# Spread maxima by one product with the unit matrix, and the PSUM places divided anew at tile 32: an attention and MLP kernel on one core

## The chip, the core and the metric

The kernel runs on one core of a Trainium2 chip. A core has TensorE (PE in the rows; PEld is its weight load), VectorE (DVE), ScalarE (ACT), GpSimd (POOL) and SyncE (SP, which here only starts transfers), each with a queue of its own in fixed order, an on-chip memory of 128 partitions, and PSUM, 8 banks of 128 x 512 fp32 values into which TensorE writes. The metric is the time of one execution on the device in microseconds (us), lower is better; the time given is the median of several executions.

## The reference, cut to what matters

```python
def _attn_ref(q, k, v, w1, b1, w2):        # q, k, v: 4 x 8 x 576 x 64
    scores = scale * np.matmul(q, k.transpose(0, 1, 3, 2))
    rel = pos[:, None] - pos[None, :]
    x = (np.log1p(abs(rel)) / np.log1p(np.maximum(pos[:, None], 1.0)))[..., None]
    bias = np.maximum(x @ w1 + b1, 0.0) @ w2          # one table for all 4 batches
    scores = scores + bias.transpose(2, 0, 1)[None, :, :, :]
    attn = softmax(scores)
    return np.matmul(attn, v)

def _moe_ref(x, w_in, w_out):               # x: 2304 x 512, w_in: 512 x 2048
    h = x @ w_in
    g = h * np.clip(h + 3.0, 0.0, 6.0) / 6.0
    return g @ w_out
```

`reference` runs the attention, lays its heads side by side and runs the MLP. The weights `w_in` and `w_out` come as 64-bit floats.

## The kernel before

**Pieces of work.** The four batches and the eight heads (four pairs) are cut into units: `(b, p, 0)` for rows 0 to 255 and `(b, p, 1)` for rows 256 to 575; a unit has four or five tiles of 128 rows by 576 columns. The main loop counts tiles with `n`, 144 in all. A tile is a product of q and k into PSUM (`qk_step`, L518 on, tile name s_ps), a VectorE pass that adds the bias and finds the row minimum (`soft_max`, L564), a ScalarE exponential (L575), and a transposition of the result. For the first 32 tiles (batches 0 and 1, rows 0 to 255, called direct) all of this is fp32 and TensorE transposes (t_ps, L623, copied out at L626). From tile 32 on the result is split into two fp16 halves (`soft_norm`, `soft_low`, hl) and a DMA transposes. At the end of a unit comes the product with v (pv_ps, L665 direct with its row sums at L676, else L711) and the copy into `x`.

**The MLP.** For each batch and row half, `ffn` (from L741) makes 16 hidden blocks (h_ps, L786, 12 products each) with ScalarE (t, L776), VectorE (t, L769), ScalarE and GpSimd (g, L763 and L765) behind them, and then 4 output blocks (o_ps, L809, 48 products each, copied out at L819). Both weight matrices are first turned from 64-bit floats into two fp16 halves by VectorE, ScalarE and GpSimd: `w_in_prep` in the first 90 us, `w_out_prep` from about 99 us. `w_out_prep` has eight chunks, and on each VectorE makes three passes over 128 x 1024 values (L265, L268, L271) and for most chunks a fourth (L141). Some chunks are staged in `z_e`, which the bias table's work also uses: a group of 16 rows of the bias table is made by `z_group` (L851 on VectorE, L855 on ScalarE), `bias_mm` (b_ps, L868) and `bias_out` (L884).

**The maxima.** Six scales are powers of two from a maximum over all 128 partitions: four for v (one per batch), one for `w_in` and one for `w_out`. `spread_max` (L145 on) finds them: a maximum per partition (m, L147, for v also masked at L150), a TensorE transposition of that column into one row (m_ps, L153), a VectorE maximum over the row (g, L155), a TensorE product of a row of ones with that one value, which gives it to all partitions (L157), and a VectorE copy (p, L160). Between these steps stand three `yield`s, so that other work is issued between. The one of `w_out` is issued at once (`drain` in `pack`). Its result gives `r_w2c` (L221), by which all 16 blocks of the first batch half's `g` are multiplied (L122 and L124) before the first output block.

**PSUM.** Two pools: places "s" of two banks each (`s_bank`, for s_ps and t_ps, and b_ps at first) and places "w" of one bank (`w_bank`, for h_ps, o_ps, pv_ps, m_ps). At first there are three s and two w. `open_banks` (from L1126) closes them and opens two s and four w over the same banks; each new place waits for the old tiles that lay there. From then on b_ps takes two w places, and `w_bank` makes sure that an output block still open is finished before the fourth claim after it.

**The order of the work.** The program is written down in source order, tile by tile: `front(n)` issues the softmax, the weights' and the bias table's steps and the MLP's steps at rates given in `CFG`. The framework that builds the program then orders the instructions of each engine by its own model of when each can start, with the source order as priority, and puts in the waits. From tile 39 on (`SWITCH`; `open_steady`, L1132) TensorE keeps the source order itself; there the steps that are left of the first MLP half are issued at once, and `open_banks` is called, since `CFG['psw']` is 99. From tile 45 on SP keeps the source order too. Tile 21 (`START`) opens the first MLP half.

Of the kernel before, what the change touches and what calls it, by code (L numbers as in the profile page):

```python
# [10 lines left out]
F32 = mybir.dt.float32  # L11
# [4 lines left out]
ALU = mybir.AluOpType  # L16
AX = mybir.AxisListType
# [7 lines left out]
NG = S // 16  # L25
CQ = 2.0 ** -25
VC = 5 * 128
CFG = {'z0': 'AD', 'gz': 12, 'z1': 'AD', 'gz2': 16, 'zeng': 'DDA', 'sg': 'P', 'wm1': 'A', 'wm2': 'RRAAAAAA', 'hl': 'AP', 'gl': 'PP', 'vm': 'A', 'g0': 8, 'rwi': 2.0, 'rw0': 0.3, 'rw1': 0.7, 'ro': 0.85, 'rb': 1.7, 'rf0': 1.3, 'rf': 2.0, 'rf1': 1.55, 'la': 6, 'gq': 2, 'gap': 0.0, 'wu': 8, 'act': 'o', 'g1': 2, 'w64': 5, 'rfo': 2.3, 'tv': 'A', 'pw': 0, 'po': 0, 'gr': 'AD', 'wb': 3, 'fb': 2, 'spn': 45, 'sw': 39, 'ws': 2, 'kn': 10, 'kw': 1, 'os': 11, 'ro2': 2.0, 'bo': 12, 'rb0': 1.5, 'psw': 99, 'xp': 0, 'mw': 2, 'he': 0}
F64_BIAS = 2.0 ** -112
F64_MAX = float(np.uint32(0x0FEFFFFF).view(np.float32))  # L30

# [2 lines left out]
def attention_moe_kernel(  # L34
# [16 lines left out]
    nc = tc.nc  # L51
    cfg = CFG
    tc.cur_priority = 10000
# [5 lines left out]
    const = ctx.enter_context(tc.tile_pool(name="const", bufs=1))  # L59
# [30 lines left out]
    def w_bank(name):  # L90

        if name == "o_ps":
            out_open[:] = [True, 0]
        elif out_open[0] and four[0]:
            while out_open[0] and out_open[1] == 3:
                next(queue[0])
            out_open[1] += 1
        return pools["ps_w"].tile([128, 512], F32, tag="w", name=name)

    open_psum(stack_p, 3, 2)  # L100
    eye_sb = const.tile([128, 128], F32, name="eye_sb")
# [2 lines left out]
    wo = big.tile([128, 2, KF, DM], F16, name="wo")  # L104
    bias_d = [dr_p.tile([H, min(128, S - i), S], F32, name=f"bias{i}") for i in range(0, S, 128)]

    ones_sb = const.tile([1, 128], F32, name="ones_sb")
    b1_sb = const.tile([128, 1], F32, name="b1_sb")
    w2_sb = const.tile([128, 32], F32, name="w2_sb")
    tq = [const.tile([128, 2, 128], F32R, name=f"tq{r}") for r in range(2)]  # L110
# [34 lines left out]
    def spread_max(parts, name, mask=False):  # L145
        m = const.tile([128, 1], F32, tag="m", bufs=2, name=f"m_{name}")
        nc.vector.tensor_reduce(out=m, in_=parts, op=ALU.max, axis=AX.X)  # L147
        if mask:
            mb = m.bitcast(U32)
            nc.vector.tensor_single_scalar(out=mb, in_=mb, scalar=0x7F800000, op=ALU.bitwise_and)  # L150
        yield
        ps = w_bank("m_ps")
        nc.tensor.transpose(ps[0:1, 0:128], m, eye_sb)  # L153
        g = const.tile([1, 1], F32, tag="gm", bufs=2, name=f"g_{name}")
        nc.vector.tensor_reduce(out=g, in_=ps[0:1, 0:128], op=ALU.max, axis=AX.X)  # L155
        yield
        nc.tensor.matmul(out=ps[:, 128:129], lhsT=ones_sb, rhs=g)  # L157
        yield
        p = const.tile([128, 1], F32, name=f"p_{name}")
        nc.vector.tensor_copy(out=p, in_=ps[:, 128:129])  # L160
        return p

    def to_pow2(p):
# [4 lines left out]
    def v_scale(b):  # L168
        parts = const.tile([128, PAIRS], F32, tag="vparts", name="vparts")
        for p in range(PAIRS):  # L170
            if b:
                t = st_p.tile([128, VC], F32, tag="vs", bufs=2, name="va")
            elif p < 2:
                t = v_t[0, p, 0] = v_p.tile([128, VC], F32, tag="vh", name="vf")
            else:
                t = v_t[0, p, 0] = st_p.tile([128, 1024], F32, tag="st", name="vf")[:, 0:VC]
            with behind():
                dq("v").dma_start(out=t, in_=vp[b, p])
            yield
            nc.vector.tensor_reduce(  # L180
                out=parts[:, p:p + 1], in_=t, op=ALU.max, axis=AX.X, apply_absolute_value=True
            )
        p = yield from spread_max(parts, f"v{b}", mask=True)
        to_pow2(p)
        s = const.tile([128, 1], F32, name=f"s_v{b}")
        nc.vector.reciprocal(out=s, in_=p)
        pscale[f"v{b}"] = (p, s)
# [28 lines left out]
    def row_ratio(p, name):  # L216
        pm = yield from spread_max(p, name)
        rm = const.tile([128, 1], F32, name=f"rm_{name}")
        nc.vector.reciprocal(out=rm, in_=pm)
        r = const.tile([128, p.shape[1]], F32, name=f"r_{name}c")  # L220
        nc.vector.tensor_scalar(out=r, in0=p, scalar1=rm, scalar2=None, op0=ALU.mult)  # L221
        pscale[name] = pm
        pscale["r" + name[1]] = r
# [807 lines left out]
    nc.sync.dma_start(out=eye_sb, in_=eye)  # L1031
    nc.sync.dma_start(out=T[:, 0:512], in_=ltab[:, 0:512])
    nc.vector.memset(cv_sb, 0.0)
    nc.vector.memset(ones_sb, 1.0)
    nc.vector.memset(c36[:, 0:1], 3.0 * CQ)
    nc.vector.memset(c36[:, 1:2], 6.0 * CQ)
    for r in range(2):
# [1 line left out]
    for cs in (slice(512, LT), slice(0, 512)):  # L1039
        nc.vector.tensor_scalar(  # L1040
            out=T[:, cs], in0=T[:, cs], scalar1=w1_sb, scalar2=None, op0=ALU.mult
# [164 lines left out]
def _layout(q, k, v, w1, b1, w2, moe_w_in, moe_w_out):  # L1206
# [7 lines left out]
    qkd = _np.concatenate([kd, qd], axis=5).reshape(Bn, PAIRS, 2, 128, HALF + 256)  # L1214
    qkd = qkd.transpose(0, 1, 3, 2, 4).reshape(Bn, PAIRS, 128, 512 + S)[:CFG["fb"]]
    rows = _np.arange(128)[:, None] + 128 * _np.arange(5)[None, :]
# [44 lines left out]
```

## Time and profile before

| | us |
|---|---|
| median of 3 executions | 697.87 (696.44 to 702.76) |
| the profiled execution | 696.51 |
| its span, first to last instruction | 694.5 |
| busy in the span: PE, PEld | 638.2, 453.0 |
| busy in the span: DVE, ACT, POOL | 485.6, 487.7, 261.7 |

Busy time of TensorE is the sum of the time in which a product runs; the granted clock (PEclk) is the share of full speed that TensorE had in a stretch, 1.00 being 2.4 GHz and 0.50 being 1.2 GHz. "Idle before" is time in which an engine did nothing ahead of an instruction, and the arrow names what ended it.

### The profile page before, as it was taken

Reading aid. Unit: us, or ns where it says so; the run is one execution under the profiler, and the core shown is the slowest. Engines: PE = TensorE matmul, PEld = TensorE weight load, DVE = VectorE, ACT = ScalarE, POOL = GpSimd, SP = SyncE. Lnnn points to the kernel's source line nnn. Section 1 sums busy time; section 2 is a strip of 40 time slices with the busy share of each in tenths; the row PEclk is TensorE's granted clock in tenths of the full one; section 3 lists DMA queues with packets and bytes.
Section 4 is the critical chain, followed back from the end, with each engine's and each line's share of the span. In section 5 each row is a group of like instructions: output and inputs, shape, how many; then the busy total and the mean of one; then the engine's idle time right before and its main releaser. Section 6 shows DMA issues by size and latency. Waiting matters only on the chain. (4 is left out here: it accounts for less than half of the span.)

```text
span 694.5 us, 15117 instructions
## 1 busy us (share of the span) xinstructions
PE 638.2 (92%) x5558; PEld 453.0 (65%) x5558; DVE 485.6 (70%) x1157; ACT 487.7 (70%) x968; POOL 261.7 (38%) x322
## 2 busy tenths in 40 slices
PE   7677899875999989999899999999999999999998
PEld 2223456653687667677788778767776777777775
DVE  7889868899846977667868887777587757710310
ACT  7987778976747987688668867886588757721620
POOL 1112125765413442246335623563365424410420
PEclk9999999998899999999999999999999999999999
DMA  8898779742893989999999899869787895400000
GB/s 294 297 329 325 268 268 337 263 130 77 230 245 93 215 229 210 236 211 206 225 258 266 167 216 191 192 142 210 169 195 136 191 177 122 91 15 29 1 10 28
DMA packets 175737, 130.13 MB, mean 187 GB/s; under 512 B 137520, under 2 KB 144944, under 8 KB 174640
## 3 DMA queue, kind: packets, MB, share of 16 engines
q1 hardware_dynamic: 165872, 113.84, 65.4%
q10 hardware_dynamic: 9792, 15.34, 7.4%
q8 instruction: 43, 0.70, 0.4%
q14 instruction: 30, 0.25, 0.1%
HBM read 77.24 MB, written 15.34 MB: 133 GB/s over the span
## 5 line engine op out<-in xcount | busy, mean ns | idle before, releaser
L786 PE MATMUL h_ps<-x,wi 128*128 128x256 f16 (+1 forms) x1536 | 200.9, 288 | 7.6 <-DVE t L769 4.0
L809 PE MATMUL o_ps<-g,wo 128*128 128x256 f16 (+1 forms) x1536 | 195.7, 286 | 1.6 <-ACT g L763 1.0
L786 PEld LDWEIGHTS <-wi 128*128 128x128 f16 x1536 | 147.7, 98 | 58.1 <-issue 18.7
L809 PEld LDWEIGHTS <-wo 128*128 128x128 f16 x1536 | 147.2, 98 | 47.2 <-issue 10.0
L765 POOL TENSOR_TENSOR g<-t,g 128x256 f16<-128x256 f32 (+1 forms) x128 | 105.5, 834 | 153.8 <-ACT g L763 152.2
L575 ACT ACTIVATE bt<-bt,sm 128x576 f32<-128x576 f32 x144 | 110.4, 767 | 41.2 <-DVE sm L564 39.4
L141 DVE SCALAR_TENSOR_TENSOR hl<-bt,sm,hl 128x576 f16<-128x576 f32 x112 | 99.1, 896 | 20.8 <-POOL hl L118 12.8
L769 DVE SCALAR_TENSOR_TENSOR t<-t,t,h_ps 128x320 f32<-128x320 f32 (+1 forms) x112 | 55.8, 515 | 47.6 <-ACT t L776 46.4
L763 ACT ACTIVATE g<-t 128x256 f16<-128x256 f32 (+1 forms) x128 | 55.4, 439 | 36.3 <-DVE t L769 35.5
L564 DVE CUSTOM_DVE_ANT_0 bt<-s_ps,bt 128x576 f32<-128x576 f32 x88 | 64.5, 750 | 22.0 <-PE s_ps L552 14.7
L118 POOL TENSOR_SCALAR hl<-bt,sm 128x576 f16<-128x576 f32 x56 | 46.7, 835 | 80.1 <-ACT bt L575 18.7
L418 POOL TENSOR_TENSOR qkl<-st,qkh 128x576 fp32r<-128x576 f32 (+2 forms) x48 | 58.5, 1238 | 37.5 <-ACT qkh L411 30.3
L776 ACT ACTIVATE t<-h_ps,t,hr 128x320 f32<-128x320 f32 (+1 forms) x112 | 64.3, 586 | 7.2 <-PE h_ps L786 2.9
L819 ACT ACTIVATE ot<-o_ps,os 128x256 f32<-128x256 f32 (+1 forms) x32 | 15.9, 497 | 64.7 <-PE o_ps L809 57.5
L868 PE MATMUL b_ps<-z_e,w_sb 128*32 128x288 f32 x448 | 45.4, 430 | 15.3 <-POOL x L699 5.9
L583 DVE TENSOR_SCALAR sm<-sm 128x1 f32<-128x1 f32 x112 | 16.9, 151 | 46.5 <-ACT bt L575 46.2
L124 ACT ACTIVATE hl<-bt,sm 128x576 f16<-128x576 f32 x56 | 43.0, 769 | 7.4 <-DVE sm L587 4.5
L851 DVE TENSOR_SCALAR z_e<-T,nbp 128x576 f32<-128x576 f32 x69 | 40.9, 638 | 1.9 <-PE b_ps L868 1.7
L884 ACT ACTIVATE bo<-b_ps,cv_sb,isc 128x288 f32<-128x288 f32 (+1 forms) x52 | 35.0, 674 | 4.3 <-DMA bias<-bo 2.4
L868 PEld LDWEIGHTS b_ps<-z_e,w_sb 128*32 128x32 f32 x448 | 14.9, 111 | 34.2 <-ACT z_e L855 6.8
L258 POOL TENSOR_SCALAR w<-w 128x1024 f32<-128x1024 f32 x8 | 12.2, 1522 | 64.3 <-ACT wo L257 58.2
L855 ACT ACTIVATE z_e<-T,bp 128x576 f32<-128x576 f32 x43 | 32.4, 769 | 5.0 <-DVE bp L1043 2.8
(132 smaller groups left out, 895.9 us busy)
## 6 DMA issues: line engine op xcount, KB each, us to landing
bt<-bias SPq DMA_DIRECT2D x36, 576.0 KB, 5.5
bias<-bo ACTq DMA_DIRECT2D x36, 288.0 KB, 5.7
w<-in_w_in_dram SPq DMA_DIRECT2D x8, 1024.0 KB, 7.1
vs<-in_vp_dram SPq DMA_DIRECT2D x24, 320.0 KB, 5.2
st<-in_qk_dram SPq DMA_DIRECT2D x16, 448.0 KB, 4.0
wo<-in_w_out_dram SPq DMA_DIRECT2D x5, 1024.0 KB, 6.6
bt<-bias SPq DMA_DIRECT2D x16, 288.0 KB, 3.3
qk<-in_qkd_dram SPq DMA_DIRECT2D x8, 544.0 KB, 9.1
```

Of the source, the lines that this page charges most:

```text
L118: nc.gpsimd.tensor_scalar(out=out, in0=full, scalar1=scale, scalar2=1.0, op0=ALU.mult, op1=ALU.mult)
L141: nc.vector.scalar_tensor_tensor(out=out, in0=full, scalar=scale, in1=high, op0=ALU.mult, op1=ALU.subtract)
L418: nc.gpsimd.tensor_sub(out=lo[:, c:c + w], in0=t[:, c:c + w], in1=hi[:, c:c + w].bitcast(F32))
L564: nc.vector.tensor_tensor_reduce(out=halves(bt), in0=ps, in1=halves(src), op0=ALU.add, op1=ALU.min, scale=-0.125, scalar=3.0e38, accum_out ...
L575: nc.scalar.activation(out=bt, in_=bt, func=AF.Exp, scale=-1.0, bias=sm[:, 0:1], accum_out=total)
L763: nc.scalar.activation(out=g[:, 0], in_=uu, func=AF.Copy)
L765: e.tensor_sub(out=g[:, 1], in0=uu, in1=g[:, 0])
L769: nc.vector.scalar_tensor_tensor(out=t_t[f], in0=t_t[f], scalar=cols(f)[2], in1=h_t.pop(f)[:, 0:n], op0=ALU.min, op1=ALU.mult,)
L776: nc.scalar.activation(out=t_t[f], in_=h_t[f][:, 0:n], func=AF.Relu, scale=cols(f)[0], bias=cols(f)[1],)
L786: nc.tensor.matmul(out=h_t[f][:, 0:n], lhsT=wi[:, a, c, f * 128:(f + 1) * 128], rhs=x[:, e, c], start=(k == 0), stop=(k == 3 * KC - 1),)
L809: nc.tensor.matmul(out=ops[:, 0:n], lhsT=wo[:, a, f, e * 128:(e + 1) * 128], rhs=g_t[f][:, r], start=(f == 0 and a == 0 and r == 0), stop= ...
L868: nc.tensor.matmul(out=pss[a][32 * k:32 * k + 32, 0:HALF], lhsT=w2_sb, rhs=z[:, a * HALF:(a + 1) * HALF],)
```

## The change

`spread_max` is left with one TensorE step: the column of maxima, repeated over 128 columns as the weights, times the unit matrix, gives every partition the whole row, and VectorE takes its maximum straight into p. Transposition, the product with ones, the copy, the row of ones and two of the three `yield`s go. `psw` becomes 32, so that `open_banks` is called in `front(32)`, seven tiles ahead of `open_steady`; TensorE's source order still begins at tile 39.

```diff
-CFG = {..., 'rb0': 1.5, 'psw': 99, 'xp': 0, 'mw': 2, 'he': 0}
+CFG = {..., 'rb0': 1.5, 'psw': 32, 'xp': 0, 'mw': 2, 'he': 0}
...
-    ones_sb = const.tile([1, 128], F32, name="ones_sb")
...
         yield
+
         ps = w_bank("m_ps")
-        nc.tensor.transpose(ps[0:1, 0:128], m, eye_sb)
-        g = const.tile([1, 1], F32, tag="gm", bufs=2, name=f"g_{name}")
-        nc.vector.tensor_reduce(out=g, in_=ps[0:1, 0:128], op=ALU.max, axis=AX.X)
-        yield
-        nc.tensor.matmul(out=ps[:, 128:129], lhsT=ones_sb, rhs=g)
-        yield
+        nc.tensor.matmul(out=ps[:, 0:128], lhsT=m.to_broadcast([128, 128]), rhs=eye_sb)
         p = const.tile([128, 1], F32, name=f"p_{name}")
-        nc.vector.tensor_copy(out=p, in_=ps[:, 128:129])
+        nc.vector.tensor_reduce(out=p, in_=ps[:, 0:128], op=ALU.max, axis=AX.X)
         return p
...
-    nc.vector.memset(ones_sb, 1.0)
```

## Rows read from the trace of the kernel before

**Rows 1.** Busy time by stretch: busy us and instructions of each engine, clock, DMA
```profile
core 0: us, PE busy (x) PEld busy (x) DVE busy (x) ACT busy (x) POOL busy (x), PEclk, DMA share, GB/s
0.00:100.00 100.00, 77.08 (x572) 36.85 (x574) 82.42 (x192) 80.22 (x127) 15.06 (x18) 1.00 0.84 305
100.00:125.00 25.00, 23.97 (x184) 15.25 (x180) 22.54 (x52) 20.22 (x41) 14.45 (x13) 1.00 0.84 293
125.00:173.00 48.00, 32.97 (x255) 23.71 (x256) 44.66 (x102) 38.96 (x73) 30.11 (x26) 0.91 0.45 147
173.00:183.20 10.20, 10.20 (x59) 4.83 (x58) 9.00 (x28) 7.40 (x12) 4.86 (x3) 0.74 1.04 287
183.20:212.00 28.80, 28.80 (x282) 22.39 (x280) 14.96 (x32) 14.15 (x25) 5.19 (x6) 1.00 0.81 211
212.00:460.00 248.00, 235.31 (x2347) 183.86 (x2339) 192.17 (x465) 195.03 (x418) 111.36 (x150) 1.00 0.92 207
460.00:694.50 234.50, 229.91 (x1879) 166.08 (x1876) 119.83 (x292) 131.74 (x277) 80.66 (x109) 1.00 0.51 106
```

**Rows 2.** TensorE in order of time, 127 to 184: start, us, line, idle before
```profile
127.45 2.77 PE L786 MATMUL h_ps<-x,wi 128*128 128x256 f16 x12
...
153.49 0.54 PE L552 MATMUL s_ps<-qkh 64*128 64x288 f32 x4
...
160.85 4.16 PE L665 MATMUL pv_ps<-atf,vf 128*64 128x256 f32 x20 [2.20 <-DVE sm L583]
...
165.53 1.48 PE L786 MATMUL h_ps<-x,wi 128*128 128x256 f16 x12
172.87 1.18 PE L868 MATMUL b_ps<-z_e,w_sb 128*32 128x288 f32 x4 [5.86 <-POOL x L699]
173.98 0.37 PE L153 MATMUL m_ps<-eye_sb,m_w 128*1 128x128 f32 x1
...
176.35 2.38 PE L786 MATMUL h_ps<-x,wi 128*128 128x256 f16 x12
178.66 0.38 PE L157 MATMUL m_ps<-g_w,ones_sb 1*128 1x1 f32 x2
...
183.23 0.50 PE L809 MATMUL o_ps<-g,wo 128*128 128x256 f16 x3
```

**Rows 3.** VectorE in order of time, 131 to 212
```profile
131.08 0.76 DVE L564 CUSTOM_DVE_ANT_0 bt<-s_ps,bt 128x576 f32<-128x576 f32 x1 [2.85 <-PE s_ps L532]
...
136.65 0.74 DVE L564 CUSTOM_DVE_ANT_0 bt<-s_ps,bt 128x576 f32<-128x576 f32 x1
...
151.71 0.75 DVE L564 CUSTOM_DVE_ANT_0 bt<-s_ps,k 128x576 f32<-128x576 f32 x1
...
172.76 0.14 DVE L147 TENSOR_REDUCE m_w<-w2p 128x1 f32<-128x8 f32 x1
...
174.81 0.47 DVE L769 SCALAR_TENSOR_TENSOR t<-t,c,h_ps 128x256 f32<-128x256 f32 x1
175.20 0.27 DVE L155 TENSOR_REDUCE g_w<-m_ps 1x1 f32<-1x128 f32 x1
...
179.07 0.16 DVE L160 COPY p_w<-m_ps 128x1 f32<-128x1 f32 x1 [0.82 <-PE m_ps L157]
...
211.32 0.76 DVE L564 CUSTOM_DVE_ANT_0 bt<-s_ps,bt 128x576 f32<-128x576 f32 x1 [8.56 <-PE s_ps L552]
```

**Rows 4.** ScalarE in order of time, at the hidden block ahead of the last
```profile
168.52 0.55 ACT L776 ACTIVATE t<-h_ps,c,hs 128x256 f32<-128x256 f32 x1
```

**Rows 5.** The instructions on m_ps: ns min/median/max, first and last start, forms
```profile
L157 PE MATMUL m_ps<-g_v,ones_sb x8: 245/256/266, 54.3 to 224.6; 1*128 1x1 f32 x8
...
L153 PE MATMUL m_ps<-eye_sb,m_v x4: 270/272/273, 52.0 to 220.4; 128*1 128x128 f32 x4
L155 DVE TENSOR_REDUCE g_v<-m_ps x4: 273/274/275, 53.4 to 222.3; 1x1 f32<-1x128 f32 x4
```

**Rows 6.** A product of a repeated column with the unit matrix, on pv_ps
```profile
L676 PE MATMUL pv_ps<-eye_sb,r_sb x64: 272/273/323, 79.5 to 191.9; 128*64 128x128 f32 x64
```

More of the change, by code (lines that the diff above doesn't have):

```diff
@@ L27 @@
 VC = 5 * 128
-CFG = {'z0': 'AD', 'gz': 12, 'z1': 'AD', 'gz2': 16, 'zeng': 'DDA', 'sg': 'P', 'wm1': 'A', 'wm2': 'RRAAAAAA', 'hl': 'AP', 'gl': 'PP', 'vm': 'A', 'g0': 8, 'rwi': 2.0, 'rw0': 0.3, 'rw1': 0.7, 'ro': 0.85, 'rb': 1.7, 'rf0': 1.3, 'rf': 2.0, 'rf1': 1.55, 'la': 6, 'gq': 2, 'gap': 0.0, 'wu': 8, 'act': 'o', 'g1': 2, 'w64': 5, 'rfo': 2.3, 'tv': 'A', 'pw': 0, 'po': 0, 'gr': 'AD', 'wb': 3, 'fb': 2, 'spn': 45, 'sw': 39, 'ws': 2, 'kn': 10, 'kw': 1, 'os': 11, 'ro2': 2.0, 'bo': 12, 'rb0': 1.5, 'psw': 99, 'xp': 0, 'mw': 2, 'he': 0}
+CFG = {'z0': 'AD', 'gz': 12, 'z1': 'AD', 'gz2': 16, 'zeng': 'DDA', 'sg': 'P', 'wm1': 'A', 'wm2': 'RRAAAAAA', 'hl': 'AP', 'gl': 'PP', 'vm': 'A', 'g0': 8, 'rwi': 2.0, 'rw0': 0.3, 'rw1': 0.7, 'ro': 0.85, 'rb': 1.7, 'rf0': 1.3, 'rf': 2.0, 'rf1': 1.55, 'la': 6, 'gq': 2, 'gap': 0.0, 'wu': 8, 'act': 'o', 'g1': 2, 'w64': 5, 'rfo': 2.3, 'tv': 'A', 'pw': 0, 'po': 0, 'gr': 'AD', 'wb': 3, 'fb': 2, 'spn': 45, 'sw': 39, 'ws': 2, 'kn': 10, 'kw': 1, 'os': 11, 'ro2': 2.0, 'bo': 12, 'rb0': 1.5, 'psw': 32, 'xp': 0, 'mw': 2, 'he': 0}
 F64_BIAS = 2.0 ** -112
```

## The prediction

> **What bounds the kernel now.** I read the busy times by stretch first, then TensorE's, VectorE's and ScalarE's instructions in order of time around the place of the change, then the instructions on m_ps. The stretches show three regimes [rows 1]. Until 100 us no engine is full: TensorE 77%, VectorE 82%, ScalarE 80% busy. From 125 to 173 us VectorE is full (44.66 of 48.00 us) while TensorE works 32.97 us and so is idle 15.0 us. From 173 us on TensorE is the bound: no idle time until 212 us, 12.7 us idle of 248 until 460, 4.6 us of 234.5 after that. So time can be won in two ways: end VectorE's full stretch sooner, or do TensorE work in the 15.0 idle us that it now does after 173 us. What merely becomes ready sooner after 173 us wins nothing, since TensorE is behind with its work there anyhow.
>
> The largest of those idle stretches is the last, 5.86 us ahead of 172.87 [rows 2]. TensorE stands at a bias-table product, b_ps; the row names GpSimd as what ended it, but the product's input is z_e, which VectorE and ScalarE write (L851, L855), and that storage is a staging place of w_out before. What else could have run? The last of the 16 hidden blocks runs at 176.35 for 2.38 us, the one before at 165.53 for 1.48 us [rows 2]. A hidden block keeps its w place until VectorE's pass has read it; for the block of 165.53, ScalarE's pass starts at 168.52 [rows 4] and VectorE's at 174.81 and takes 0.47 us [rows 3]. The other place belongs to the product with v of 160.85 and then to m_ps [rows 2]. So with two w places the last block can't start before about 175.3: a wait on storage, not on data.
>
> **The change part by part.**
>
> *One product for two.* A spread now has one TensorE pass of 0.27 us for the transposition (L153) and two of about 0.256 us for the product with ones (L157: eight records for four maxima) [rows 5]. The new product is like the row sums' one, a repeated column times the unit matrix, 128 columns: 64 records for 32 uses, so two passes of 0.273 us [rows 6]. TensorE goes from 0.27 + 2 x 0.256 = 0.78 to 2 x 0.273 = 0.55 us, 0.23 us less by durations that partly overlap; between no gain and 0.5 us less. VectorE keeps one maximum over 128 values (0.274 us [rows 5]; over 128 partitions instead of one I take the same, as its length in columns is the same) and loses the copy, 0.16 us [rows 3]. Only the maxima after 173 us stand in a TensorE-bound stretch, that of w_out and the last of v: 2 x 0.23 = **0.5 us**.
>
> The trip is shortened much more than the work. For w_out the column of maxima is there at 172.9, the transposition runs at 173.98, VectorE's maximum at 175.20, the second product only at 178.66 (behind a bias product and the hidden block of 176.35), the copy at 179.07 [rows 2, 3]. With one product p is there with the maximum, at about 175.5: 179.2 - 175.5 = 3.7 us sooner. The first output block starts at 183.23 [rows 2] and needs this scale. But TensorE is not idle between 173.00 and 183.20 [rows 1]: an output block that may start 3.7 us sooner changes places with bias and score products that must run too. I count 0 for it, and up to 3.7 us if that cover goes. In the first 100 us there are three more of these trips; nothing there ends on them, and the weights' passes that fill VectorE don't wait for them. I count 0, with 1 us either way for work that is ordered anew.
>
> The Trainium skill, Perfetto Trace Analysis, section Transposes, speaks against this edit: a logical transposition should use the transposing form, which skips the arithmetic, and not a standard product. The trace agrees on the price (one pass against two). By that rule alone six maxima would cost 6 x 0.27 = 1.6 us more; by the rows the second product that goes with it more than pays this.
>
> *Four w places from tile 32.* VectorE's score pass at 136.65 is the 33rd, that of tile 32 [rows 3], so the new places cover most of the stretch from 125 to 173. The last hidden block no longer waits for VectorE's pass on the block before: it can follow at 167.0 in the idle 5.86 us and leaves the full stretch after 173: **2.4 us** [rows 2]. The other idle waits of TensorE before it close too, but only as far as VectorE reads the results sooner, and VectorE is full; each hidden block costs it the same 0.47 us whenever it comes. What VectorE still has is idle time: 3.3 us between 125 and 173 [rows 1], of which 2.85 us lie ahead of 131.08, where it waits for score products [rows 3] that stand behind a hidden block at a lowered clock (2.77 us against 1.48 [rows 2]). A maximum of v holds one of the two w places around there. No row says that this wait goes; it is worth 0 to 2.85 us and I take the middle, **1.4 us**.
>
> *The clock.* From 173.0 to 183.2 TensorE was granted 0.74 of its clock [rows 1], after the idle 5.86 us; that is 10.2 x 0.26 = 2.7 us of lost speed, of which 0.9 is in the hidden block already counted. A block of 1.5 us in the gap need not keep the clock up: between 0 and 1.8 us, I take 0.
>
> *Three s places become two.* The score products of two tiles of the split kind go together, so two places hold just one pair. Does a third serve here? The products of the pair at 153.49 start after VectorE's second pass on the pair before (151.71, 0.75 us) [rows 2, 3]: two would do there. The bias table leaves the s places at the same time. I count 0; 0 to 9 us lost (below).
>
> Sum, against the profiled execution's 696.51 us (span 694.5 and 2.0 around it): 0.5 + 2.4 + 1.4 = 4.3, so 692.2. That execution is 1.4 us under the median of the three; on the median's footing **693.6 us**, 0.6% less. What is late next is TensorE itself: after 183.2 there is nothing in the change.
>
> **The rivals.**
>
> *Nothing moves.* VectorE's chain through the eight chunks of w_out ends where it ended, the freed gap is taken by other work, and the builder's new order gives back the two or three us. For it: VectorE is 93% busy from 125 to 173 [rows 1], and TensorE's order before tile 39 is the builder's, not the source's, so that more places needn't be used. Against it: the last hidden block's wait is plainly one for a place. Time: 697.87 less 0.5, about 697.4.
>
> *The places were the bound.* Then all bubbles go as far as VectorE's own idle time allows: 2.5 us from 100 to 125 and 3.3 from 125 to 173 [rows 1], plus the hidden block's 2.4 and the clock's 1.8: 10.0, with the 0.5 of the spreads 10.5, so 687.4. For it: TensorE's 15.0 idle us beside only two w places. Against it: some waits end on VectorE's small sums (2.20 us ahead of 160.85 [rows 2]), which no place shortens. The Trainium skill, Perfetto Trace Analysis, section Optimization Strategy, reads repeated gaps on the engine that should be saturated as a possible lack of storage for the next tile; the trace agrees for the last gap alone.
>
> *Slower: output blocks run ahead of the scores.* With four places open, a fourth claim on a w place after an output block closes that block at once, and bias groups now take two claims each. Four output blocks may then be issued ahead of the scores of tiles 38 and 39 in the order that TensorE keeps, while s has no third place to run scores ahead. VectorE then waits as it does now behind the output blocks, 8.56 us ahead of 211.32 [rows 3]; today TensorE's own work covers that. It costs from the point on where the next units' products with v wait for tiles that VectorE got too late: once, the same 8.56 us on TensorE, less the 0.5: 697.9 + 8.1 = 706.0. Against it: only two or three bias groups fall between tiles 35 and 39, and the work left of the first half is issued in one piece at tile 39 in both kernels.
>
> **How the numbers follow.** Forecast 0.42, its own range 690 to 696.5 (all of the clock and of the 2.85 us at the one end, the hidden block alone less one us at the other). Nothing moves 0.26, the places were the bound 0.20, slower 0.12. About what a measurement of this kernel tells from no change is 1%, here 7.0 us: under 690.9 faster, over 704.9 slower. Faster: the places' 0.20 and 0.04 of the forecast's lower end, 0.24. Slower: 0.10, since a part of that case stops short of 704.9. The same: 0.66. The range goes from 685, which leaves out a quarter of the places' case, to 702.5, which leaves out most of the slower one: some 0.15 outside.
>
> **What would show it.** Right: the last hidden block follows the one before within some 2 us; TensorE's idle time from 125 to 173 falls from 15.0 to about 11 to 12; the first output block starts at 176 to 181 and the last of the first half ends 4 us sooner; the trip of w_out's maximum, column to p, is under 4 us against 6.3; two passes of 0.27 us per spread. Wrong: the output blocks start sooner and the stretch after them ends no sooner (nothing moves); VectorE idle over 3 us between tiles 32 and 39, or the first output blocks ahead of the scores of tile 38 and TensorE idle over 17.3 us after 212 (slower); TensorE's idle time before 173 under 8 us (the places were the bound); a change of several us before 120 us, which no term here has.

## The result, and the profile after

The changed kernel took 703.43 us (median of 11 executions, 698.08 to 708.75) beside 697.37 (11 executions, 695.35 to 702.76) for the kernel before on the same chip: ratio 1.0069, interval 1.0046 to 1.0091. The ratios are taken over the fast executions alone (the one of 708.75 us is left out as slow) and are not the quotients of the medians, which would give 1.0087 here. The forecast was 693.6 with a range up to 702.5. It is slower, by 0.7%, where 0.6% faster was forecast. A repetition gave 704.17 and 1.0075 (1.0042 to 1.0108). The profiled execution of the changed kernel took 703.6 us, with a span of 701.8 (before 696.51 and 694.5), so it is an ordinary one. That of the kernel before had a high clock: mean granted clock 0.990, where 29 executions of it beside the first experiments had 0.978 to 0.990, median 0.985. The changed kernel's eleven had 0.963 to 0.987, median 0.973, and the profiled one 0.973. So a part of what the two profiles differ by is the execution and not the kernel.

The busy times by stretch, cut at about the same points of the work as [rows 1]: the last hidden block of the first call of the MLP now ends at 167.3, its first output block starts at 177.1, and the second call's first hidden block at 214.5 (212.3 before). The columns are those of [rows 1].

```profile
core 0: us, PE busy (x) PEld busy (x) DVE busy (x) ACT busy (x) POOL busy (x), PEclk, DMA share, GB/s
0.00:100.00 100.00, 79.55 (x553) 36.99 (x555) 86.18 (x192) 79.75 (x125) 15.03 (x18) 0.95 0.84 304
100.00:125.00 25.00, 23.34 (x184) 15.33 (x180) 19.26 (x47) 20.84 (x41) 12.83 (x12) 1.00 0.85 306
125.00:167.30 42.30, 35.05 (x262) 25.15 (x262) 40.18 (x84) 33.16 (x62) 30.66 (x24) 0.92 0.43 149
167.30:177.10 9.80, 4.01 (x18) 3.43 (x19) 9.72 (x29) 6.79 (x15) 2.65 (x5) 0.63 0.53 109
177.10:214.50 37.40, 35.35 (x326) 24.91 (x326) 19.22 (x50) 20.18 (x38) 5.60 (x7) 0.96 0.87 224
214.50:467.30 252.80, 239.41 (x2342) 186.07 (x2338) 192.94 (x462) 196.01 (x419) 111.30 (x150) 0.98 0.92 203
467.30:701.80 234.50, 229.97 (x1881) 166.12 (x1877) 119.70 (x292) 131.77 (x277) 81.39 (x109) 1.00 0.50 107
```

And the first part of the page, busy time of each engine over the span:

```profile
PE 646.7 (92%) x5552; PEld 458.0 (65%) x5552; DVE 487.2 (69%) x1150; ACT 488.5 (70%) x972; POOL 259.5 (37%) x322
```

The last 234.5 us are the same to the tenth. In these two profiles everything is lost ahead of them: 2.5 us by 214.5 (212.0 before), 4.8 more by 467.3 (460.0 before). And it isn't lost as idle time. Over the whole span TensorE is idle 701.8 - 646.7 = 55.1 us, 1.2 less than before (694.5 - 638.2 = 56.3). It is busy 8.5 us more, though the six spreads have three passes before and two now, six fewer in all. From 214.5 to 467.3 the idle time goes from 12.69 to 13.39 us and the busy time from 235.31 to 239.41, for the same products (records missing from a trace apart). What lengthens a product is the granted clock, in column PEclk: 0.95, 0.96 and 0.98 where [rows 1] have 1.00. How the loss is spread isn't fixed: a second profile of the changed kernel (span 702.0) has the second call at 211.1 us, sooner than before, and loses all of it after that.

TensorE in order of time around the end of the first half's hidden blocks, to be held against [rows 2]:

```profile
164.77 0.27 PE L781 MATMUL h_ps<-x,wi 128*128 128x256 f16 x1
165.48 0.49 PE L153 MATMUL m_ps<-eye_sb,m_w 128*128 128x128 f32 x2 [0.44 <-DVE m_w L146]
165.81 1.47 PE L781 MATMUL h_ps<-x,wi 128*128 128x256 f16 x12
173.09 1.30 PE L618 MATMUL t_ps<-eye_sb,bt 128*128 128x128 f32 x5 [5.81 <-DVE sm L559]
174.32 0.85 PE L547 MATMUL s_ps<-qkh 64*128 64x288 f32 x2
...
177.07 1.46 PE L804 MATMUL o_ps<-g,wo 128*128 128x256 f16 x6
```

The last hidden block does follow at once, 10.5 us sooner than the 176.35 of [rows 2]. But the gap of 5.86 us ahead of it hasn't closed. It stands behind it now, 5.81 us, ahead of a transposition that waits until VectorE's score pass of tile 34 has freed an s place. That pass, at 151.03 us before, comes in VectorE's order only at 172.19. The kernel before:

```profile
151.03 0.75 DVE L564 CUSTOM_DVE_ANT_0 bt<-s_ps,k 128x576 f32<-128x576 f32 x1
```

The changed kernel's VectorE in order of time over the same stretch, and its two long waits among the first output blocks:

```profile
165.30 0.13 DVE L146 TENSOR_REDUCE m_w<-w2p 128x1 f32<-128x8 f32 x1
165.36 1.63 DVE L846 TENSOR_SCALAR z_e<-T,nbp 128x576 f32<-128x576 f32 x2
166.91 1.76 DVE L140 SCALAR_TENSOR_TENSOR wo<-cu,w2s,wo 128x1024 f16<-128x1024 f32 x1
...
169.72 1.96 DVE L140 SCALAR_TENSOR_TENSOR hl<-bt,sm,hl 128x576 f16<-128x576 f32 x2
171.60 0.28 DVE L155 TENSOR_REDUCE p_w<-m_ps 128x1 f32<-128x128 f32 x1
...
172.19 0.75 DVE L559 CUSTOM_DVE_ANT_0 bt<-s_ps,k 128x576 f32<-128x576 f32 x1
...
193.37 0.82 DVE L175 TENSOR_REDUCE vparts<-va 128x1 f32<-128x640 f32 x1 [6.94 <-DMA va<-in_vp_dram]
...
213.46 0.76 DVE L559 CUSTOM_DVE_ANT_0 bt<-s_ps,bt 128x576 f32<-128x576 f32 x1 [7.69 <-PE s_ps L547]
```

The trip of w_out's maximum, column to p, takes 171.60 + 0.28 - 165.30 = 6.6 us, as long as the old one with two products and a copy (6.5 by the same count [rows 3]). TensorE has the product done by 166.0; VectorE's maximum starts 5.6 us after that, queued behind VectorE's other passes.

The instructions on m_ps, beside [rows 5]:

```profile
L153 PE MATMUL m_ps<-eye_sb,m_v x8: 275/275/581, 50.7 to 222.8; 128*128 128x128 f32 x8
L155 DVE TENSOR_REDUCE p_v<-m_ps x4: 280/286/287, 52.7 to 225.9; 128x1 f32<-128x128 f32 x4
```

Two passes of 0.275 us and a maximum of 0.286, as worked out; the 0.581 is a pass at the lower clock.

One place shows what the clock does by itself. A score pass near 345 us waits for VectorE in both kernels, equally long. First the kernel before, then the changed one:

```profile
343.33 0.53 PE L552 MATMUL s_ps<-qkh 64*128 64x288 f32 x3 [2.33 <-DVE sm L564]
...
344.31 1.17 PE L711 MATMUL pv_ps<-at,vh 128*64 128x256 f16 x18
345.32 0.71 PE L711 MATMUL pv_ps<-at,vl 128*64 128x256 f16 x10
345.96 1.26 PE L809 MATMUL o_ps<-g,wo 128*128 128x256 f16 x10
```

```profile
347.72 0.85 PE L547 MATMUL s_ps<-qkh 64*128 64x288 f32 x3 [2.34 <-DVE sm L559]
...
349.45 2.13 PE L706 MATMUL pv_ps<-at,vh 128*64 128x256 f16 x18
351.37 1.28 PE L706 MATMUL pv_ps<-at,vl 128*64 128x256 f16 x10
352.59 4.83 PE L804 MATMUL o_ps<-g,wo 128*128 128x256 f16 x36
```

From the end of the wait to the output block: 2.63 us before, 4.87 after. The trace has the changed kernel at 1.2 GHz for 6.8 us from 347.3 and the kernel before at 2.4 GHz throughout. The second profile of the changed kernel has it again: a wait of 2.33 us, and 6.8 us at 1.2 GHz from 347.4. But the length of the wait doesn't decide it. Of the 20 profiles of this work 18 have this wait at this product (not the two with a filler, below), always 2.32 to 2.34 us long; in 11 of them a stretch at 1.2 GHz begins within 2 us of its end, in 7 none does.

### The profile page after: what moved, and what is told of

Same layout as the page of the kernel before. It is cut to its first block, busy times and chain, and to the rows that moved or that the text cites. A ratio compares the mean times of both kernels' runs of the same rounds, so it can differ in the third digit from the quotient of the medians.

```text
span 701.8 us, 15111 instructions
## 1 busy us (share of the span) xinstructions
PE 646.7 (92%) x5552; PEld 458.0 (65%) x5552; DVE 487.2 (69%) x1150; ACT 488.5 (70%) x972; POOL 259.5 (37%) x322
## 5 line engine op out<-in xcount | busy, mean ns | idle before, releaser
L117 POOL TENSOR_SCALAR hl<-bt,sm 128x576 f16<-128x576 f32 x56 | 45.2, 807 | 96.4 <-DVE sm L582 22.8
L879 ACT ACTIVATE bo<-b_ps,cv_sb,isc 128x288 f32<-128x288 f32 (+1 forms) x56 | 36.5, 653 | 4.0 <-DMA bias<-bo 2.4
L618 PE MATMUL t_ps<-eye_sb,bt 128*128 128x128 f32 x160 | 25.6, 294 | 12.9 <-DVE sm L559 8.0
```

Of the source, the lines that this page charges most:

```text
L117: nc.gpsimd.tensor_scalar(out=out, in0=full, scalar1=scale, scalar2=1.0, op0=ALU.mult, op1=ALU.mult)
```

## The experiments

The theories in the order in which they came: P, the places do the harm; S, the spreads do; C, the clock; T, the third s place is missed; W, four w places let the MLP run ahead of the scores; L, the shorter trip gains and the early maxima harm; N, TensorE is behind and a sooner scale buys nothing; and last O, what decides is the order that the builder draws for the engines, and any redrawing of it costs.

**The changed kernel again**, and **one part alone.**

```diff
# spreads only                      # places only: the old spread_max, and
-'psw': 32                          -'psw': 99
+'psw': 99                          +'psw': 32
```

> The changed kernel once more, for its scatter and a second trace. All theories: 702 to 705. Theory C (what the time follows is TensorE's granted clock, which falls at other places from run to run): its mean clock is 0.97 to 0.98 again, but the stretch at half clock near 347 us may be missing, and tile 72's lag behind the kernel before is then 4 us and not 7.

> The new spread alone, places opened at tile 39 as before (psw 99). Theory P (the loss comes from the places at tile 32): 696 to 698, ratio 0.998 to 1.001, and tile 36's score pass at 155 to 160 us as before. Theory S (the loss comes from the shorter spreads, which change the order of the work from the first 60 us on): 701 to 704, ratio 1.005 to 1.009, with tile 32's score pass 4 to 6 us late (141 to 143 us).

> The old spread, with two s and four w places from tile 32. Theory P: 701 to 704, ratio 1.005 to 1.009, tile 36's score pass late (170 to 180 us against 156.3) and TensorE at half clock about 170 to 180 us. Theory S: 696 to 698, ratio 0.998 to 1.001.

Measured: 704.17 (above); spreads alone 702.29, ratio 1.0057 (1.0024 to 1.0089); places alone 709.30, 1.0162 (1.0125 to 1.0200). Both parts alone are slower, and the sum of the two, 2.2%, is three times what they do together. So neither part has a price of its own that could be added up. The number of S came true for the spreads alone (701 to 704); for the places alone 709.30 lies outside both theories. In the second profile of the changed kernel the fall near 347 us isn't missing, as C thought it might be, and tile 72's score pass is as late as in the first (359.26 and 359.12, for 351.77 before).

**Opening the places later,** at tile 36 and 34 instead of 32, with the new spread and with the old one.

```diff
-'psw': 32
+'psw': 36      # or 34; and 36 with the old spread_max
```

> The changed kernel with the places opened at tile 36 instead of 32. Theory P: less of the loss, 698 to 701, since fewer tiles lack the third s place. Theory S: 702 to 704 as the changed kernel.

> The changed kernel with the places opened at tile 34 instead of 32. Theory T: tile 34's score pass is at 150 to 153 us again (172.19 in the changed kernel), since the pair of tiles 34 and 35 is claimed before the opening; the time is that of psw 36, 700 to 703. Theory W: as the changed kernel, 703 to 705.

> The old spread with the places opened at tile 36 instead of 32. Theory T (what the early opening costs is the third s place while tile 31's transposition and the score pair of tiles 34 and 35 want places at once): most of the 11 us of the places alone goes, 697 to 701, and tile 34's score pass is back at 150 to 153 us. Theory W (the cost is in what four w places let run ahead, the output blocks and the bias groups): 705 to 709 still, since output blocks and bias groups come only after tile 36.

Measured: 701.90, 1.0049 (1.0024 to 1.0073); 700.59, 1.0040 (1.0015 to 1.0065); with the old spread 705.86, 1.0112 (1.0084 to 1.0140). With 36 and 34 the score pass of tile 34 is on time again (151.78 with 36), so that the delay of 21 us at tiles 34 to 37 does come from opening at 32, where s loses its third place. T is right about the delay and wrong about the time: without it 0.40 and 0.49% of the 0.69% are still lost, and a changed kernel that has the delay (7 warm-up products, below; tile 34 at 171.47) loses 0.32%. The numbers settle nothing between T and W: with 34 the time is T's (700 to 703), with the old spread and 36 it is W's (705 to 709). P and S miss 701.90 both.

**The new spread for some of the maxima only.**

```diff
     yield
+    if name == "w2":                       # or: if name in ("v0", "v1", "w1"):
+        ps = w_bank("m_ps")
+        nc.tensor.matmul(out=ps[:, 0:128], lhsT=m.to_broadcast([128, 128]), rhs=eye_sb)
+        p = const.tile([128, 1], F32, name=f"p_{name}")
+        nc.vector.tensor_reduce(out=p, in_=ps[:, 0:128], op=ALU.max, axis=AX.X)
+        return p
```

> The kernel before (places at tile 39), with the one product for the maximum of w_out alone; the other five maxima in the old way. Theory L (the trip on the path is the gain, and the early maxima do the harm by a new order of VectorE): 694 to 697.5, ratio 0.994 to 0.999, first output block 3 to 4 us sooner than 183.2. Theory N (TensorE is behind with its work after 173 us, so the sooner scale buys nothing): 697 to 699, ratio 0.999 to 1.002.

> The kernel before (places at tile 39), with the one product for the maxima of w_in and of v of the first two batches alone, all of them before 100 us. Theory L: it carries the loss of the spreads, 701 to 703, ratio 1.004 to 1.008, with tile 24's score pass at 116 to 117 us (111.95 before) and the first w_out chunk's maximum at 95 us (99.84 before). Theory N, or the loss being in the later maxima: 697 to 699.

Measured: 699.84, 1.0031 (1.0010 to 1.0052), and 701.26, 1.0052 (1.0031 to 1.0072). The first half of L falls: with w_out's spread alone its maximum is there 2.5 us sooner (176.7 for 179.2), the first output block starts at 183.06 for 183.23, and nothing is gained; the 697 to 699 of N was 0.8 us too low. The second half of L came true in its number (701 to 703) and in its mark (tile 24's score pass at 116.86). That this is no price of the early maxima themselves is seen from the redrawings below: the first hidden block starts at 102.7 here for 97.1 before, but at 103.4 to 107.6 in three kernels without any of the change (6, 10 and 9 warm-up products), and at 96.4 in one that holds all of it (7). The first of these two kernels changes one small chain and redraws little, some 15 rows of TensorE's order where the whole change redraws 277. All eight changed kernels up to here were slower, whatever they held. That suggested O.

**Redrawing the order of the kernel before.** The framework orders each engine's instructions by its own model of when each can start; a product more or less at the very start moves all of that.

```diff
-'wu': 8       # warm-up products ahead of all other work
+'wu': 9       # or 7, or 10
```

> The kernel before, nothing of the change in it, with one more of the eight warm-up products at its very start (0.45 us each there, 3.59 us for eight). The builder lays every engine's instructions out anew: 210 rows of TensorE's order and 380 of VectorE's differ from before's, as many as the change made (277 and 340). Theory H (the harm is the change's own: the place count, the maxima's timing): 697.4 to 698.9 us, the same as before within 0.2 per cent. Theory O (the order of before is a good draw out of many, and any redrawing costs, whatever it was for): 700 to 705 us, 0.3 to 1.0 per cent slower, as all eight changed kernels were. Rival Z (redrawings go both ways): below 696.

> The kernel before with one warm-up product less at its start, nothing of the change in it; 89 rows of TensorE's order and 285 of VectorE's differ from before's. H: 697.0 to 698.5. O: 700 to 705. Z: below 696.

> The kernel before with two warm-up products more at its start; 254 rows of TensorE's order and 331 of VectorE's differ. H: 697.6 to 699.1. O: 700 to 705, and with the two others a mean near 702 to 703, so that the changed kernel (703.4) stands in the middle of redrawings that hold nothing of the change. Z: at least one of the three below 696.

Measured: 714.92, 1.0234 (1.0190 to 1.0278); 702.93, 1.0066 (1.0042 to 1.0089); 706.68, 1.0133 (1.0088 to 1.0178). These kernels hold nothing of the change, and are as slow as the changed one or slower. O's own number, 700 to 705, was right for one of them and too low for two. A warm-up product takes 0.45 us, so its own time is no explanation of 5 to 17 us. That it acts through the order alone isn't shown by itself: the granted clock of the first 20 us is 1.00 in all 20 profiles, but no run redraws the order with every product left as it was. H, harm of the change's own, has lost its ground: 5 us is the smallest of what a mere redrawing costs. The worst of them and the kernel before, up to the end of the first half and in the stretch after it:

```profile
0.00:225.40 225.40, 182.53 (x1344) 108.88 (x1344) 179.61 (x404) 161.49 (x274) 62.70 (x64) 0.92 0.72 239
225.40:475.60 250.20, 238.06 (x2349) 185.59 (x2343) 191.61 (x461) 195.50 (x419) 111.24 (x150) 0.99 0.92 205
```

```profile
0.00:212.00 212.00, 173.02 (x1343) 103.03 (x1343) 173.58 (x401) 160.95 (x274) 69.66 (x64) 0.97 0.76 254
212.00:460.00 248.00, 235.31 (x2347) 183.86 (x2339) 192.17 (x465) 195.03 (x418) 111.36 (x150) 1.00 0.92 207
```

Of the 13.4 us that it loses by the end of the first half, 9.5 are longer busy time at a clock of 0.92 for 0.97 (0.45 of it the product more), and 3.9 are idle time. This is where the time stands, not yet its cause: in most of this stretch TensorE isn't the bound [rows 1], and VectorE is busy 6.0 us longer too (179.61 for 173.58).

**A filler for the clock.** In the changed kernel, products on data that always lies ready fill the wait near 347 us; nobody reads what they write.

```diff
+                    if n == 69 and k + a + j == 0:
+                        for _ in range(34):
+                            nc.tensor.matmul(
+                                out=o_at[0][:, 384:512],       # second try: s_t[n][:, 1, 384:512]
+                                lhsT=wi[:, 0, 0, 0:128], rhs=wi[:, 0, 0, 0:128],
+                            )
```

> The changed kernel with 34 products of 128 columns, on data that always lies ready, put between the first and the second product of the score pass near 345 us, where TensorE waits 2.34 us for VectorE and the granted clock then falls to 1.2 GHz for 6.8 us; they write unused columns of the open output block's place and are read by nobody. TensorE's order is otherwise the changed kernel's. About 2 us of products lie inside a wait of 2.3 us. Theory C (the clock's fall is a part of the loss, about 3 us there): no fall near 347 us, the lag behind before that jumps from 4.5 to 7.4 us there stays near 5, and the time is 2 to 3 us under the changed kernel's: 700.5 to 701.5. Rival D (the fall follows from something else, or the time is given back at the next wait): 702.5 to 704.5.

> The filler again, in the changed kernel near 347 us, now written into unused columns of the score place that TensorE has just been given, so that the 34 products wait for nobody (the first filler wrote into a place whose reader it had to wait for, 3.58 us, and then ran 3.11 us at the half clock). TensorE's order is otherwise the changed kernel's; 24 rows of VectorE's order around it differ. C (the clock's fall is about 3 us of the loss): no fall at 347 us, and 700.5 to 701.5 us. D (it follows from something else or is given back): 702.5 to 704.5, with the lag at 360 us the same 7.4.

The first was a miss of mine: 706.75, 1.0112 (1.0080 to 1.0143). The output block whose place the fillers write into had just ended, so they wait for ScalarE's copy of it, and the clock falls at 351.6, while they run (3.11 us, for 2.07 in the second try):

```profile
350.78 3.11 PE L554 MATMUL o_ps<-wi 128*128 128x128 f16 x34 [3.58 <-ACT ot L822]
353.82 0.85 PE L548 MATMUL s_ps<-qkh 64*128 64x288 f32 x3
```

The second did what it should in its place:

```profile
346.05 2.07 PE L553 MATMUL s_ps<-wi 128*128 128x128 f16 x34
348.44 0.53 PE L547 MATMUL s_ps<-qkh 64*128 64x288 f32 x3 [0.32 <-DVE sm L565]
...
349.43 1.17 PE L712 MATMUL pv_ps<-at,vh 128*64 128x256 f16 x18
350.44 0.71 PE L712 MATMUL pv_ps<-at,vl 128*64 128x256 f16 x10
351.08 4.10 PE L810 MATMUL o_ps<-g,wo 128*128 128x256 f16 x36
```

No fall there. Against the changed kernel's profiled execution this one is 0.7 us later just ahead of the wait (the score product before it at 345.72 for 344.99) and 1.5 us sooner at the output block (351.08 for 352.59): 2.2 us gained at the one place. At the end 0.8 us are left. But its median is 704.47, 1.0096 (1.0059 to 1.0132): not under the changed kernel's. C's number, 700.5 to 701.5, fell, and D's, 702.5 to 704.5, holds. That a fall costs some 2 us where it meets products is seen in this execution. That the filler prevented it isn't shown, since 7 of the 18 profiles without a filler have no fall at this wait either. What this one fall is worth in the median isn't shown.

**Redrawing the changed kernel, and the pairs.** The same edit of `wu` in the changed kernel, and the two runs that complete five pairs.

```diff
-'wu': 8
+'wu': 7      # or 9, 6 and 10 in the changed kernel; 6 in the kernel before
```

> The changed kernel with one warm-up product less: 117 rows of TensorE's order and 237 of VectorE's redrawn, the change itself kept. The same redrawing of the kernel before gave 702.9, and 706.7 and 714.9 with two others. O (the drawn order decides, the change itself does nothing): between 700 and 712, as the redrawn kernels before. V (the change itself is worth 3 to 5 us, only against a lucky order it doesn't show): 699 to 704, and the three redrawn changed kernels with a mean 4 us or more under the 708.2 of the three redrawn ones before. H (the change itself harms by 5 us on top of the drawing): above 708.

> The changed kernel with one warm-up product more, whose like cost the kernel before 17 us (714.9): 218 rows of TensorE's order and 282 of VectorE's redrawn. O: 700 to 715, V: 699 to 704, H: above 710.

> The changed kernel with two warm-up products less: 152 rows of TensorE's order and 342 of VectorE's redrawn. O: 700 to 715, V: 699 to 704, H: above 710. If one of the three redrawn changed kernels is under 698, the change can be faster than the kernel before with another order.

> The kernel before with two warm-up products less, the pair of the changed kernel's 708.7 (1.0158). Up to here the pairs with 8, 7 and 9 warm-up products stand at 1.0069, 1.0032 and 1.0168 for the changed kernel against 1, 1.0066 and 1.0234 for the one before: differences of +0.7, -0.3 and -0.7 per cent. O (the drawn order decides, the change itself is worth nothing that shows): 700 to 712, either side of 708.7. V (the change itself gains 3 us or more): above 711. H (it harms by 3 us or more): below 705, with the next one's opposite.

> The changed kernel with two warm-up products more, the pair of the kernel before's 706.7 (1.0133). O: 700 to 712, either side of 706.7, and the mean of the five pairs' differences within 0.4 per cent of nothing. V: below 703.5. H: above 710.

Measured, as ratios to the kernel before of the same chip run (us in brackets):

| warm-up products | without the change | with the change | difference |
|---|---|---|---|
| 8 | 1 | 1.0069 (703.43) | +0.7% |
| 7 | 1.0066 (702.93) | 1.0032 (700.45) | -0.3% |
| 9 | 1.0234 (714.92) | 1.0168 (710.54) | -0.7% |
| 6 | 1.0157 (710.04) | 1.0158 (708.67) | 0.0% |
| 10 | 1.0133 (706.68) | 1.0200 (713.18) | +0.7% |

The mean difference is +0.1%, and with a scatter of 0.6% over five pairs its own interval is some 0.7% to either side. The warm-up count moves the time by up to 2.3%, in no order of its size. O stands as far as this: what the change itself is worth is too small to be seen beside the order that is drawn with it. The pairs don't show that it is worth nothing. The forecast of 0.6% less lies inside that interval, and so does a harm of 0.7%. V fell with its mark: the three redrawn changed kernels have a mean of 706.6, 1.6 us under the 708.2 of the redrawn ones before, where it wanted 4. H's numbers came true for the changed kernel with 9 and 10 products (710.54 and 713.18, above 710), and not with 6 or 7; with 10 the time lies above O's 700 to 712. The kernel before has the lowest median of the ten, and 8 is the count that it came with, so that the first pair may set a chosen draw against a chance one; the other four alone have a mean of -0.1%. One changed kernel (7 products, 1.0032, 0.9997 to 1.0066) can't be told from it; none is faster.

**Where the draws differ.** From the rows of TensorE in order of time: the start of the first hidden block of the first, second and fourth call of the MLP, and what is left of the span after that; and from the head of each profile TensorE's busy time and the rest of the span (us, profiled executions).

```
                        call 1  call 2  call 4  after it   busy   idle
before                    97.1   212.3   361.5     333.0   638.2  56.3
changed                  103.3   214.5   368.8     333.0   646.7  55.1
changed, again           102.8   211.1   369.0     333.0   645.4  56.6
spreads only             103.4   212.0   363.4     333.6   642.0  55.0
changed, places at 34    102.7   209.0   362.5     333.8   643.9  52.4
before, 9 warm-ups       107.6   225.7   376.8     333.3   650.2  59.9
before, 7 warm-ups        96.9   217.6   369.8     333.0   647.2  55.6
changed, 7 warm-ups       96.4   212.1   363.4     333.3   641.5  55.2
changed, 9 warm-ups      107.8   223.7   377.2     333.3   648.9  61.6
```

After the fourth call's start all take the same 333 to 334 us. Up to the second call's start, in the stretch whose order on TensorE is mostly the builder's (the source order begins at tile 39), these draws spread over 17 us (209.0 to 225.7); from the second call to the fourth they take 149.2 to 157.9, the kernel before least. The two profiles of the changed kernel are 3.4 us apart at the second call, so that a single row here is good to a few us only. And not all of the loss stands where the order differs. In the traces of this table, compared by operation and tile name, the order of TensorE, VectorE, ScalarE and GpSimd is the same from 253 us of the kernel before on; yet the changed kernel loses 5.1 of its 7.3 us between the second and the fourth call, and its repetition more than all of them. Between the two calls the clock of the changed kernel's first profile falls at 296 and at 347 us, and that of the kernel before nowhere. How an order that differs only earlier leads to that isn't shown. Over all 19 profiles of other kernels (the changed one twice), TensorE's busy time is 2.5 to 12.0 us longer than before's, and the idle time between 4.2 us shorter and 6.4 longer.

## Why the prediction was wrong

**What was right.** The parts of the change did locally what was worked out: two passes of 0.275 us; the last hidden block right behind the one before it; the first output block at 177.07, inside 176 to 181; TensorE's idle time from 125 to 173 us at 48.00 - 35.05 = 12.95, down from 15.03, if not to 11 to 12. The mark of "nothing moves" came true as well: the output blocks start 6.2 us sooner (177.07 for 183.23), and the stretch after them ends 2.2 us later (214.5 for 212.3); in the second profile they start 9.8 us sooner (173.44), and of that 1.2 us are left at the second call. With the places at 34 the second call starts 3.3 us sooner than before (209.0 for 212.3), near the 4.3 of the sum, and it is given back by the fourth; but two executions of one kernel are as far apart there, so that this is no proof of the sum.

**The step that failed** is the frame of the sum: "After 183.2 there is nothing in the change", and for the first 100 us "I count 0, with 1 us either way for work that is ordered anew". The sum priced the edited instructions within the old order. But the change redraws the order of the whole built program, 277 rows of TensorE's and 340 of VectorE's, and that term is worth +5 to +17 us by the redrawings that hold nothing else. I had named it, in the rival "nothing moves" ("the builder's new order gives back the two or three us"), and there had mis-sized it and bounded it on the wrong side: as a gain given back, or 1 us either way. The mark "a change of several us before 120 us, which no term here has" came true: the first hidden block starts at 103.3 instead of 97.1, and at 102.8 in the second profile. "After 183.2 there is nothing in the change" failed by itself too, by the 5.1 us between the second call and the fourth.

**The 2.4 us of the hidden block.** It left the stretch after 173, as forecast, and nothing was won. TensorE's gap went behind it, 5.81 us for 5.86; with the clock at 0.63 in the stretch that holds it (0.74 in [rows 1] for the stretch that follows the old gap).

**The 1.4 us of VectorE's idle time.** Between 125 and 173 VectorE is now idle 48.00 - 45.88 = 2.1 us for 3.3: 1.2 us, nearly the forecast.

```profile
125.00:173.00 48.00, 35.05 (x262) 25.15 (x262) 45.88 (x93) 35.91 (x67) 32.03 (x27) 0.90 0.42 139
```

Whether it was kept can't be read at the second call (214.5 and 211.1 in the two profiles, 212.3 before). Behind it VectorE waits 6.94 us ahead of 193.37, where the kernel before waits 1.13 and 2.36 in the same passes; the row names a transfer of v, which no term of the sum has.

**The clock, counted 0 with 0 to 1.8 us gained.** Wrong in sign. In the profiled execution the loss stands as busy time, 8.5 us more, and not as idle time, 1.2 us less. The mean clock alone doesn't give the time, though: the changed kernel with 7 warm-up products has the same one (0.972 for 0.973) and is busy 5.2 us less, with a span 5.1 us shorter. That a drawn order alone, without the change's two parts, brings such a clock is shown by the redrawings (busy 9.0 and 12.0 us longer for two of them). Which waits of an order bring a fall isn't settled: of 18 equal ones at the same product 11 did.

**The third s place, counted 0 with 0 to 9 us lost.** At the split tiles from which the prediction judged, two places do. But from 32 on there are direct tiles in flight, whose transpositions take s places as well; opening at 32 delayed tiles 34 to 37 by 21 us. That was the wrong row to judge from. By the runs with 34 and 36 it costs 0.2 to 0.3% of the time, 1.4 to 2 us, if that difference isn't a draw too; the changed kernel with 7 warm-up products has the same delay and loses 0.32% in all.

**The trip of w_out's maximum.** Forecast under 4 us, measured 6.6: I took the maximum to start when the product ends, and it is queued on a VectorE that is full. Its 0 us of worth was right in that a sooner scale buys nothing: that spread alone has it 2.5 us sooner and gave 1.0031.

**The slower rival,** output blocks ahead of the scores, 706.0, has its marks: VectorE idle 6.94 us ahead of 193.37, the first output block at 177.07 ahead of tile 38's scores, and TensorE idle 17.9 us after 212.

```profile
192.46 0.53 PE L547 MATMUL s_ps<-qkh 64*128 64x288 f32 x4
```

But the long wait is for a transfer of v and not for scores, the one for tile 40's scores is shorter than before (7.69 for 8.56 us), and the idle time after 212 is 0.6 us above the 17.3 of before. Kernels that never open the places early (spreads alone, redrawn before) lose as much. So it isn't needed for the loss; what it adds in this kernel isn't shown.

Of the two rules that were weighed, the first is that of the Trainium skill, Perfetto Trace Analysis, section Transposes: a logical transposition should use the transposing form and not an ordinary product. The trace bears out that the ordinary product costs more, 2 x 0.275 us for 0.272; the two passes of 0.256 that go outweigh this. The second is that of the Trainium skill, Perfetto Trace Analysis, section Optimization Strategy: repeated gaps on the engine that should be full may come from too little storage for the next tile. The trace agrees for the hidden block's wait, which went; the gap moved behind it, 5.81 us for 5.86, and the whole wasn't shortened.

## What to carry to other kernels

Where a framework orders the engines' instructions itself, a small edit can redraw hundreds of rows far from it, and a measured difference then holds a difference of two draws. Before an effect of under 2% is put down to an edit, redraw the old and the new kernel by an edit that does next to nothing (here one warm-up product more or less) and compare the pairs; count how many are needed, as five pairs left 0.7% to either side here. When busy time grows while the instructions stay the same, read the granted clock of each stretch before searching for a wait.

## What the runs showed of the hardware that was not expected

But for a product or two at the start, the same products took TensorE 638.2 us of busy time in the kernel before and 650.2 with one warm-up product more (mean granted clock 0.990 and 0.968), so that longer products carry more of the difference between these two kernels, 12.0 us, than TensorE's idle time does, 3.6 us. Waits of 2.32 to 2.34 us at one and the same product were followed by a stretch at 1.2 GHz in 11 profiles of 18, and left the clock at 2.4 GHz in 7; both profiles of the changed kernel have 6.8 us of it, the nine others less. And 34 products without use, 2.07 us in a wait of that length, stood where the clock then stayed up, and what follows came 2 us sooner in that execution; the median of the runs was no lower, and without them the clock stays up in some kernels too.
